# Strided attention into two feed-forward layers, one core: weights split in another way, and a new plan of the order

## Chip, cores, metric

One core of a Trainium2 chip runs the whole program. The metric is device time in microseconds for one execution.

## What is computed

Attention with 4 batches, 8 heads, 576 positions and head size 64: four heads look at the 32 latest positions, four at every 32nd earlier one. Its output, 2304 tokens of 512 numbers, goes through two feed-forward layers with 2048 hidden units each.

```python
scores = scale * np.matmul(q, k.transpose(0, 1, 3, 2))
mask_local = (rel >= 0) & (rel < stride)
mask_strided = (rel >= 0) & (pos[None, :] % stride == pos[:, None] % stride)
scores = np.where(masks[None, :, :, :], scores, -1000000000.0)
attn = np.exp(scores - np.max(scores, axis=-1, keepdims=True))
attn = attn / (np.sum(attn, axis=-1, keepdims=True) + 1e-09)
x = np.matmul(attn, v)                    # then laid out as 2304 x 512
h = x @ w_in;  x = (h * np.clip(h + 3.0, 0.0, 6.0) / 6.0) @ w_out
h = x @ w_in2; y = (h * np.tanh(np.log1p(np.exp(h)))) @ w_out2
```

Everything is float32; the weights are handed over as float64.

## The kernel before

**An order worked out beforehand.** The body adds its operations to a plan (class Plan, L103): each with an engine or a choice of engines, a cost in nanoseconds, what it depends on, and a due time. Plan.run (L171) is a list scheduler: again and again it takes the operation that can start first, and of those that can start at the same time the one that is due first (L199). Where an operation may run on several engines it takes the one on which it ends first, after a handicap (BIAS, FIRST_BIAS: 0 for GpSimd, 4000 ns for VectorE). Operations with a `lock` on an engine do not overlap in the plan (L192, L211). Then the instructions are issued in planned order (L862), so each engine works through its own queue in that order, whatever the true times are. The DMA loads are one queue, issued by SP.

**Fillers.** Up to FILL_UNTIL (L69, 20974 ns) of planned time, gaps of TensorE are filled with matmuls on zeros of FILL = 128 columns (fill, L155; L855 to L859), written to a bank that nothing uses then. Plan.stream (L143) halves TensorE's planned rate after stretches with few columns.

**Attention.** Work goes by pairs of heads, 4 a batch, 16 in all (attend, L467). For a pair: q, k and v are loaded (load_pair, L438; SP at L446 and L460); 76 small matmuls make the scores in two banks (L490); VectorE adds the masks while scaling, into tile e (L503); then the maximum (L529), its subtraction (L530, GpSimd or VectorE), exp on ScalarE (L531), the sum (L532), its reciprocal (L534), the product (L535, GpSimd or VectorE); TensorE transposes e (L543, L546: 8 matmuls); copies to pt; 72 small matmuls with v (L574); and the result is split into xh (ScalarE, L292) and xl (VectorE, L600). float32 matmuls count double in the trace: "x76" is 38 in the code. There are N_E = 2 tiles e, so the scores of a pair wait for the transposes of the pair but one before (e_free, L476, L512). The strided masks are twelve small loads on SP (L422).

**Feed-forward.** Products are made to full precision of three matmuls on rounded operands (mm3, L693): high x low parts and high x high. Tokens are in blocks of 512, 512, 512, 256 and 512; hidden units in 16 chunks of 128 a layer; GROUPS splits the chunks into groups of 4, 6, 6 and 6, 5, 5. A step is one chunk on one block: 4 mm3 into h, the nonlinearity (hard_swish L700, mish L712), its split into gh (L292) and gl (L792, GpSimd or VectorE), and 4 mm3 into the sums y. Block 0 needs batch 0 of the attention, block 1 batches 0 and 1, and so on, so attention runs in between in the first group.

**Weights.** A chunk has two halves (in and out), 64 halves in all, each 128 x 512 float64. decode (L630) makes from each a rounded float32 part w(0) and a rest w(1): sign away (L651, ScalarE or VectorE), clamp (L658), shift of the high word by 3 (L662), merge of sign and exponent (L667), rounding copy to w(0) (L292), then the power of two (L673), the low 9 bits of the high word (L677), those joined with the low word (L681), and their product with the power as w(1) (L685). There are 3 raw tiles, 3 wa, 2 wm and 8 slots for finished chunks (6 until attention has ended).

**Due times** (L360 to L367, L606 to L627): START is when the feed-forward part is to begin, UNIT the time that it allows for a pair in between, EARLY_X how long before its first use a batch is due, HALF_PACE the least distance between two halves' due times.

## Time and profile before

| | us |
|---|---|
| median of 3 runs | 890.5 (889.73 to 892.34) |
| profiled execution | 890.85 |
| its span, first to last instruction | 889.0 |

| engine | busy us | share | instructions |
|---|---|---|---|
| TensorE, matmuls | 871.2 | 98% | 6448 |
| VectorE | 567.7 | 64% | 978 |
| ScalarE | 492.4 | 55% | 923 |
| GpSimd | 265.3 | 30% | 223 |

Busy time of TensorE counts the fillers and matmuls at half clock in full. A row of a timeline is a run of like instructions of one engine: start, length, how many, and in square brackets the idle time before it with what ended it. "issue" there means that nothing which the profile shows was waited for. Times in the table of groups are busy time and the mean of one in nanoseconds.

### The profile page before, as it was taken

To read this page: it belongs to the slowest core of one execution; us is meant where nothing else is said; L and a number is where in the kernel's file an instruction comes from. 1 tells how busy PE (TensorE), PEld (TensorE's weight loads), DVE (VectorE), ACT (ScalarE), POOL (GpSimd) and SP (SyncE) were. 2 spreads that over 40 slices of the span, in tenths; PEclk is the share of its full clock that TensorE was granted. 3 is DMA by queue.
4 is the path that set the end of the run, shared out by engine and by line. 5 is a ranking of instruction groups with operands and counts; after the bars stand their busy time and mean duration, and the time that the engine had idled before them with its cause. 6 is when DMAs were issued, how large, how long until landed. Compare 5 with 4: busy or idle time off the path is not lost.

```text
span 889.0 us, 15898 instructions
## 1 busy us (share of the span) xinstructions
PE 871.2 (98%) x6448; PEld 730.8 (82%) x6448; DVE 567.7 (64%) x978; ACT 492.4 (55%) x923; POOL 265.3 (30%) x223
## 2 busy tenths in 40 slices
PE   9698999999999999999999999999999999999998
PEld 8476777888888988888898888888888888888887
DVE  6668667888521479822168888346888867555564
ACT  2344554654222244433245877788887778666674
POOL 3243434222222222244262432222222222222222
PEclk9689999999999999999999999999999999999999
DMA  7956653323100022300003112000221100000112
GB/s 231 240 167 172 184 148 90 93 94 115 48 1 1 1 72 94 103 17 1 1 25 94 48 48 72 0 2 24 71 72 48 48 1 1 0 36 13 48 47 72
DMA packets 20441, 58.73 MB, mean 66 GB/s; under 512 B 3344, under 2 KB 6032, under 8 KB 20368
## 3 DMA queue, kind: packets, MB, share of 16 engines
q1 hardware_dynamic: 20368, 57.72, 21.9%
q8 instruction: 50, 0.82, 0.4%
q14 instruction: 23, 0.19, 0.1%
HBM read 52.99 MB, written 4.72 MB: 65 GB/s over the span
## 4 chain that ended last, share of the span: by engine, by line
PE 93%; issue 2%; DMA 2%; DVE 1%; SPq 1%; POOL 1%; ACT 0%; POOLq 0%
PE bank L696 30%; PE bank L697 29%; PE bank L698 29%; PE bank L574 2%; PE bank L490 1%; DMA y<-in_qkv_dram 1%; DMA v<-in_qkv_dram 1%; PE bank L543 1%; PE bank L546 1%; POOL e L535 0%; SPq L422 0%; SPq L647 0%; POOL gl L792 0%; DVE y L830 0%; DVE wa L673 0%
## 5 line engine op out<-in xcount | busy, mean ns | idle before, releaser
L792 POOL TENSOR_TENSOR gl<-t,gh 128x512 fp32r<-128x512 f32 (+1 forms) x160 | 198.7, 1243 | 539.4 <-ACT gh L292 496.2
L696 PE MATMUL bank<-xh,w 128*128 128x512 f32 (+1 forms) x640 | 238.5, 373 | 0.5 <-DVE e L503 0.5
L696 PE MATMUL bank<-gh,w 128*128 128x512 f32 (+1 forms) x640 | 237.6, 371 | 0.0
L697 PE MATMUL bank<-xl,w 128*128 128x512 f32 (+1 forms) x640 | 237.4, 371 | 0.0
L697 PE MATMUL bank<-gl,w 128*128 128x512 f32 (+1 forms) x640 | 236.3, 369 | 0.8 <-POOL gl L792 0.8
L698 PE MATMUL bank<-xh,w 128*128 128x512 f32 (+1 forms) x640 | 236.2, 369 | 0.0
L698 PE MATMUL bank<-gh,w 128*128 128x512 f32 (+1 forms) x640 | 235.5, 368 | 0.0
L696 PEld LDWEIGHTS bank<-xh,w 128*128 128x128 f32 x640 | 121.0, 189 | 22.7 <-issue 1.2
L696 PEld LDWEIGHTS bank<-gh,w 128*128 128x128 f32 x640 | 120.4, 188 | 21.8 <-issue 0.7
L698 PEld LDWEIGHTS bank<-xh,w 128*128 128x128 f32 x640 | 121.0, 189 | 20.8
L698 PEld LDWEIGHTS bank<-gh,w 128*128 128x128 f32 x640 | 120.4, 188 | 20.8 <-issue 0.3
L697 PEld LDWEIGHTS bank<-xl,w 128*128 128x128 f32 x640 | 121.1, 189 | 19.9 <-DVE xl L600 0.5
L697 PEld LDWEIGHTS bank<-gl,w 128*128 128x128 f32 x640 | 120.5, 188 | 20.5 <-POOL gl L792 1.2
L707 DVE SCALAR_TENSOR_TENSOR t<-t,bank 128x512 f32<-128x512 f32 (+1 forms) x80 | 50.6, 634 | 135.1 <-ACT t L704 134.8
L704 ACT ACTIVATE t<-bank 128x512 f32<-128x512 f32 (+1 forms) x80 | 44.2, 555 | 149.9 <-PE bank L698 149.8
L292 ACT CAST gh<-t 128x512 fp32r<-128x512 f32 (+1 forms) x160 | 91.3, 572 | 42.8 <-DVE t L707 23.2
L735 DVE SCALAR_TENSOR_TENSOR t<-t,seed 128x512 f32<-128x512 f32 (+1 forms) x80 | 70.9, 887 | 62.8 <-ACT seed L724 62.0
L740 DVE SCALAR_TENSOR_TENSOR t<-t,seed 128x512 f32<-128x512 f32 (+1 forms) x80 | 58.4, 730 | 41.4 <-ACT t L737 41.2
L737 ACT ACTIVATE t<-t,offset 128x512 f32<-128x512 f32 (+1 forms) x80 | 54.4, 680 | 49.9 <-DVE t L735 49.7
L830 DVE TENSOR_TENSOR y<-bank,y 128x512 f32<-128x512 f32 (+1 forms) x80 | 49.7, 636 | 22.3 <-PE bank L698 21.4
L728 ACT ACTIVATE t<-bank 128x512 f32<-128x512 f32 (+1 forms) x80 | 44.3, 554 | 29.6 <-PE bank L698 27.3
L651 ACT ACTIVATE wa<-raw 128x512 f32<-128x512 f32 x64 | 43.1, 673 | 28.1 <-DMA raw<-in_wts_dram 19.0
(51 smaller groups left out, 839.2 us busy)
## 6 DMA issues: line engine op xcount, KB each, us to landing
raw<-in_wts_dram SPq DMA_DIRECT2D x64, 512.0 KB, 3.7
qk<-in_qkv_dram SPq DMA_DIRECT2D x15, 576.0 KB, 5.2
v<-in_qkv_dram SPq DMA_DIRECT2D x22, 256.0 KB, 4.7
out_dram<-y SPq DMA_DIRECT2D x16, 256.0 KB, 2.0
v<-in_qkv_dram SPq DMA_DIRECT2D x8, 288.0 KB, 5.2
y<-in_qkv_dram SPq DMA_DIRECT2D x1, 576.0 KB, 8.4
y<-in_qkv_dram SPq DMA_DIRECT2D x2, 256.0 KB, 7.9
out_dram<-y SPq DMA_DIRECT2D x4, 128.0 KB, 1.8
```

The lines of the kernel that those rows point to most:

```text
L292: nc.scalar.copy(out, src)
L696: nc.tensor.matmul(o, a[:, 1], high, start=first, stop=False)
L697: nc.tensor.matmul(o, a[:, 0], low, start=False, stop=False)
L698: nc.tensor.matmul(o, a[:, 0], high, start=False, stop=last)
L704: o = add("act", act_ns(n, True), lambda: nc.scalar.activation(t, h(), AF.Relu, bias=0.5, scale=1.0 / 6.0), [prod, free])
L707: lambda: nc.vector.scalar_tensor_tensor(t, t, 1.0, h(), ALU.min, ALU.mult), [o], frees=s.h,
L728: o = add("act", act_ns(n, True), lambda: nc.scalar.activation(t, h(), AF.Tanh, scale=0.5), [prod, free])
L735: lambda: nc.vector.scalar_tensor_tensor(t, t, 4.0, seed(), ALU.add, ALU.mult), [o], lock=("dve",),
L737: o = add("act", act_ns(n), lambda: nc.scalar.activation(t, t, AF.Square, bias=offset, scale=scale), [o])
L740: lambda: nc.vector.scalar_tensor_tensor(t, t, more, seed(), ALU.add, ALU.mult), [o], lock=("dve",),
L792: lambda eng, gh=gh, gl=gl, t=t: engines[eng].tensor_tensor(gl, t, gh.bitcast(F32), ALU.subtract),
L830: lambda y=y, src=src: nc.vector.tensor_tensor(y(), src(), y(), ALU.add), [op, *before], due=due, frees=bank,
```

## The change

1. decode: the mask of the rest is 0x3FFFFFFF instead of 0x3FFFF000, so the merged value keeps 20 bits of mantissa; w(0) is its rounding copy as before. The rest w(1) is now (merged value - w(0)) + low word x 2^-52 x power. Seven VectorE instructions become four (shift, merge, power, product); the clamp, the subtraction and the addition may run on GpSimd or VectorE.
2. The plan knows TensorE's instruction supply (late): instructions come in pieces of PIECE = 256, each is asked for at a fixed place and arrives SUPPLY = 6000 ns later; an operation that would run out is planned later. A filler counts 4 instructions, mm3 6, scores 152, transposes 16, values 144.
3. Fillers have 512 columns, until 60000 ns of planned time, and a tile of zeros of their own (640 columns).
4. The twelve strided mask loads are issued by ScalarE, due at 3000 ns.
5. N_E is 4; the scores no longer wait for a free e (the mask additions still do), and two of the e tiles get their unused columns cleared by GpSimd.
6. UNIT 1800 to 1200, HALF_PACE 7500 to 6263, EARLY_X 11000 to 8000.

```diff
-N_QKV, N_E, N_PT = 2, 2, 2
+N_QKV, N_E, N_PT = 2, 4, 2
-UNIT = 1800
-HALF_PACE = 7500
-EARLY_W, EARLY_G, EARLY_X = 8224, 12000, 11000
+UNIT = 1200
+HALF_PACE = 6263
+EARLY_W, EARLY_G, EARLY_X = 8224, 12000, 8000
-FILL, FILL_UNTIL = 128, 20974
+FILL, FILL_UNTIL = 512, 60000
+PIECE, ASKED, AHEAD, SUPPLY = 256, 140, 308, 6000
...
+    def late(self, t, op):
+        done, s = self.counted, 0.0
+        first, n = done[-1][0], op.count or 6
+        k = max(0, -(-(first - ASKED - AHEAD) // PIECE))
+        while (asked := ASKED + k * PIECE) + AHEAD < first + n:
+            if asked < first:
+                i = bisect.bisect_left(done, (asked, 0.0))
+                s = max(s, done[i][1] + SUPPLY - t - max(0, asked + AHEAD - first) / n * op.cost)
+            k += 1
+        return s
...
                     t = at[e]
+                    if e == "pe":
+                        t += self.late(t, op)
...
+    zeros = ap_.tile([P, P + FILL], F32, name="zeros")
...
-            return add("dma", 460, lambda: nc.sync.dma_start(mk_str[rows, slots], src))
+            return add("act", 420, lambda: nc.scalar.dma_start(mk_str[rows, slots], src), due=3000)
...
-        done = []
+        done = [add("pool", 150, lambda e=e: nc.gpsimd.memset(e[:, :, WS:], 0.0), due=12000) for e in e_t[NPAIR // 2:]]
...
-        s_op = add("pe", 900, scores, [src.qk, *e_free], bank=both)
+        s_op = add("pe", 900, scores, [src.qk], bank=both)
+        s_op.count = 4 * (4 * NB + 2)
...
         o = add(
-            "dve", dve_ns(DM / 2),
-            lambda: nc.vector.tensor_scalar(a, a, TINY, HUGE, ALU.max, ALU.min), [o], lock=("dve",),
+            None, {"dve": dve_ns(DM / 2), "pool": 50 + 1.05 * DM},
+            lambda eng: engines[eng].tensor_scalar(a, a, TINY, HUGE, ALU.max, ALU.min), [o], lock=("dve", "pool"),
         )
         o = add(
             "dve", dve_ns(DM / 2),
-            lambda: nc.vector.tensor_scalar(ai, ai, 3, 0x3FFFF000, ALU.logical_shift_left, ALU.bitwise_and),
+            lambda: nc.vector.tensor_scalar(ai, ai, 3, 0x3FFFFFFF, ALU.logical_shift_left, ALU.bitwise_and),
             [o], lock=("dve",),
         )
-        hi = add(
+        whole = add(
             "dve", dve_ns(DM),
             lambda: nc.vector.scalar_tensor_tensor(ai, high, 0xC0000000, ai, ALU.bitwise_and, ALU.bitwise_or),
             [o], lock=("dve",),
         )
-        o = add(None, copy_ns(DM), lambda eng: copy(eng, w(0), a), [hi, *old_w], lock=("dve",))
-        power = add(
-            "dve", dve_ns(DM / 2),
-            lambda: nc.vector.tensor_scalar(ai, ai, 0xFF800000, None, ALU.bitwise_and), [o], lock=("dve",),
-        )
+        hi = add(None, copy_ns(DM), lambda eng: copy(eng, w(0), a), [whole, *old_w], lock=("dve",))
         o = add(
             "dve", dve_ns(DM / 2),
-            lambda: nc.vector.tensor_scalar(resti, high, 0x1FF, None, ALU.bitwise_and), [load, old_m], lock=("dve",),
+            lambda: nc.vector.tensor_scalar(resti, ai, 0xFF800000, None, ALU.bitwise_and), [whole, old_m], lock=("dve",),
+        )
+        tail = add(
+            "dve", dve_ns(DM),
+            lambda: nc.vector.scalar_tensor_tensor(rest, low, 2.0 ** -52, rest, ALU.mult, ALU.mult), [o], lock=("dve",),
         )
         o = add(
-            "dve", dve_ns(DM),
-            lambda: nc.vector.scalar_tensor_tensor(rest, resti, 2.0 ** 32, low, ALU.mult, ALU.add), [o], lock=("dve",),
+            None, plain_ns(DM),
+            lambda eng: engines[eng].tensor_tensor(a, a, w(0).bitcast(F32), ALU.subtract), [hi, o], lock=("dve", "pool"),
         )
         lo = add(
-            "dve", dve_ns(DM),
-            lambda: nc.vector.scalar_tensor_tensor(w(1), rest, 2.0 ** -52, a, ALU.mult, ALU.mult),
-            [o, power, *old_w], lock=("dve",),
+            None, plain_ns(DM),
+            lambda eng: engines[eng].tensor_tensor(w(1), a, rest, ALU.add), [o, tail, *old_w], lock=("dve", "pool"),
         )
-        w_ops.append({"raw": [hi, o], "end": lo})
+        w_ops.append({"raw": [whole, tail], "end": lo})
...
-    zeros = t_t[0]
-    cleared = add("dve", 520, lambda: nc.vector.memset(zeros[:, :2 * P], 0.0), due=0)
+    cleared = add("dve", 520, lambda: nc.vector.memset(zeros, 0.0), due=0)
```

## Rows read from the trace of the kernel before

**Rows 1.** Page, slices of the span, granted clock of TensorE in tenths

```profile
PEclk9689999999999999999999999999999999999999
```

**Rows 2.** Stretches: length, busy us (instructions) of five engines, clock, DMA share, GB/s

```profile
0.00:29.00 29.00, 22.80 (x487) 21.00 (x491) 17.48 (x39) 7.69 (x14) 9.88 (x15) 0.98 0.81 227
29.00:52.90 23.90, 20.86 (x428) 16.11 (x425) 13.72 (x31) 9.41 (x22) 3.51 (x3) 0.53 0.71 201
52.90:100.00 47.10, 42.85 (x890) 33.41 (x889) 37.11 (x79) 25.89 (x57) 21.43 (x17) 1.00 0.64 185
...
100.00:884.00 784.00, 784.00 (x4652) 659.72 (x4651) 498.19 (x827) 449.44 (x832) 230.49 (x188) 1.00 0.16 49
```

**Rows 3.** Timeline of TensorE, saturated stretch: start, length, instructions

```profile
103.52 0.39 PE L696 MATMUL bank<-gh,w 128*128 128x512 f32 x1
...
104.20 0.60 PE L543 MATMUL bank<-mk,e 128*128 128x128 f32 x4
...
105.10 1.00 PE L490 MATMUL bank<-qk 64*32 64x54 f32 x76
...
106.93 1.25 PE L574 MATMUL bank<-pt,v 64*64 64x32 f32 x72
```

**Rows 4.** Timeline of TensorE, first 50 us

```profile
9.40 9.87 PE L857 MATMUL bank<-t 128*128 128x128 f32 x86
...
20.00 1.00 PE L490 MATMUL bank<-y 64*32 64x54 f32 x76
...
24.45 0.88 PE L574 MATMUL bank<-pt,v 64*64 64x32 f32 x42 [0.97 <-DMA v<-in_qkv_dram]
28.81 2.88 PE L574 MATMUL bank<-pt,v 64*64 64x32 f32 x98 [3.47 <-issue]
...
33.91 1.12 PE L543 MATMUL bank<-mk,e 128*128 128x128 f32 x4 [0.28 <-POOL e L535]
...
41.81 0.42 PE L574 MATMUL bank<-pt,y 54*64 54x32 f32 x2 [2.75 <-issue]
...
46.73 2.14 PE L574 MATMUL bank<-pt,v 54*64 54x32 f32 x72
```

**Rows 5.** Timeline of TensorE, around 70 us

```profile
69.08 0.31 PE L574 MATMUL bank<-pt,v 64*64 64x32 f32 x6 [1.26 <-issue]
69.90 0.50 PE L696 MATMUL bank<-xh,w 128*128 128x512 f32 x1 [0.51 <-DVE e L503]
```

**Rows 6.** Chain of waits (a landing), timelines of SP and ScalarE, first 20 us

```profile
3.12 8.38 DMA y<-in_qkv_dram
...
3.62 10.07 SPq L422 DMA_DIRECT2D mk_str<-in_masks_dram  x12
...
15.35 3.73 SPq L460 DMA_DIRECT2D v<-in_qkv_dram  x6
...
13.23 0.68 ACT L531 ACTIVATE e<-e 128x576 f32<-128x576 f32 x1 [2.85 <-POOL e L530]
```

**Rows 7.** Groups by line on VectorE, 0 to 100 us: three of decode's seven

```profile
L673 DVE TENSOR_SCALAR wa<-wa 128x512 uint32<-128x512 uint32 x8 | 6.5, 811 | 0.7 <-ACT w L292 0.7
...
L681 DVE SCALAR_TENSOR_TENSOR wm<-wm,raw 128x512 f32<-128x512 uint32 x8 | 5.5, 694 | 0.0
...
L662 DVE TENSOR_SCALAR wa<-wa 128x512 uint32<-128x512 uint32 x9 | 3.8, 417 | 0.0
```

**Rows 8.** Groups by line on GpSimd, whole span

```profile
L792 POOL TENSOR_TENSOR gl<-t,gh 128x512 fp32r<-128x512 f32 (+1 forms) x160 | 198.7, 1243 | 539.4 <-ACT gh L292 496.2 <-issue 34.7 <-PE bank L697 8.6
...
L726 POOL TENSOR_SCALAR seed<-seed 128x512 f32<-128x512 f32 x2 | 1.2, 618 | 5.2 <-ACT seed L731 5.2
```

**Rows 9.** Timelines of VectorE and GpSimd, 60 to 70 us

```profile
63.49 1.38 DVE L673 TENSOR_SCALAR wa<-wa 128x512 uint32<-128x512 uint32 x1
...
65.85 0.63 DVE L685 SCALAR_TENSOR_TENSOR w<-wm,wa 128x512 fp32r<-128x512 f32 x1
...
63.05 1.53 POOL L535 TENSOR_TENSOR e<-e,sum 128x576 f32<-128x576 f32 x1 [2.22 <-DVE sum L534]
```

More of the change, by code (lines that the diff above doesn't have):

```diff
@@ L1 @@
+import bisect
 import concourse.bass as bass
@@ L77 @@
 class Op:
-    __slots__ = ("engine", "costs", "cost", "emit", "deps", "due", "banks", "frees", "start", "end", "left", "users", "rows", "lock")
+    __slots__ = ("engine", "costs", "cost", "emit", "deps", "due", "banks", "frees", "start", "end", "left", "users", "rows", "lock", "count")
     def __init__(self, costs, emit, deps, due, bank, frees, lock=""):
@@ L92, in __init__ @@
         self.rows = 1.0
+        self.count = 0
         self.lock = lock
@@ L168, in fill @@
             t = free_bank[n] = op.end
+            n = self.counted[-1][0]
+            self.counted.extend([(n, op.start), (n + 4, op.end)])
         return done
     def run(self):
-        self.columns = {}
+        self.columns, self.counted = {}, [(0, 0.0)]
         free = dict.fromkeys(self.AFTER, ORIGIN)
@@ L210, in run @@
             free[e] = op.end
+            if e == "pe":
+                n = self.counted[-1][0]
+                self.counted.extend([(n, t), (n + (op.count or 6), op.end)])
             if e in op.lock:
@@ L852, in attention_then_two_ffns @@
     add("dve", 60, lambda: nc.vector.memset(offset, STEP[1]), due=1000)
-    zeros = t_t[0]
-    cleared = add("dve", 520, lambda: nc.vector.memset(zeros[:, :2 * P], 0.0), due=0)
+    cleared = add("dve", 520, lambda: nc.vector.memset(zeros, 0.0), due=0)
     plan.filler = cleared, 3 + 4 * FILL / 2.4, lambda n: nc.tensor.matmul(
-        banks[n][:, :FILL], zeros[:, :P], zeros[:, P:P + FILL], start=True, stop=True
+        banks[n][:, :FILL], zeros[:, :P], zeros[:, P:], start=True, stop=True
     )
```

4 lines of the change are left out of this document (3 added, 1 removed).

## Prediction

> **What bounds the kernel now.** I read the slices of the page first: the granted clock of TensorE drops in the second and third slice and nowhere else [rows 1]. The table by stretches comes next: from 100 to 884 us TensorE is busy for every microsecond at full clock, with VectorE and GpSimd at 64% and 29% [rows 2]. Whatever is taken off another engine there is worth nothing unless it makes TensorE wait. The question is how much useful TensorE work is done in the first 100 us.
>
> That needs prices at full clock, read where TensorE is saturated [rows 3]: the transposes of a pair take 0.90 us from start to start, a triple of 512-wide matmuls 0.68, and by their own rows the scores 1.00 and the values 1.25, so 3.15 us a pair. By 52.9 us the timeline holds six score groups (6.0), four transposes (3.6), four values (5.0) and six triples (4.1): 18.7 us of useful work, 34.2 lost. From 52.9 to 100 us TensorE is idle for 47.10 - 42.85 = 4.3 us [rows 2]. The loss is 38.5 us in all, and the forecast is what part of it comes back.
>
> Where it goes stands in the timeline of TensorE [rows 4]. Until 19 us fillers run, because the first pairs are in their softmax. The scores of pair 2 start at 20.00, right behind the transposes of pair 0, whose e tile they need (N_E is 2); those of pair 3 stand behind the transposes of pair 1. Then the values wait 0.97 us for v, and twice, 3.47 and 2.75 us, for "issue", which is no semaphore at all. The clock falls to 1.2 GHz with the first of these two and is back at 52.9 us (mean 0.53 in between) [rows 2]. The values of pair 3 end near 49 us, and only then does the feed-forward part run in earnest.
>
> What is "issue"? 478, 733 and 1242 matmuls stand before the rows that end such waits at 28.81, 41.81 and 69.08 [rows 4, 5]. With a weight load each, that is instruction 956, 1466 and 2484: steps of 510 and 1018, near twice and four times 256. All fall into groups of short matmuls, some 75 in 1.2 us. TensorE runs out of instructions there, at the pieces that the new planner calls PIECE. The Trainium skill ("Runtime: NRT & Kernel Launch", Instruction fetch mechanics) says that instructions come in blocks of 256 and that crossing a block's boundary is "mostly hidden". The spacing agrees with the block; the 3.47 and 2.75 us do not agree with hidden. By that rule the supply term below would be nothing, and rival B is what is left.
>
> **The change part by part.**
>
> Supply in the plan: the two early waits, 6.2 us, lie on the path; the plan now puts other work or a filler in front of such an instruction. Only the order is changed, so a piece that comes later than the planned 6 us still stalls TensorE. From instruction 652, in the scores at 20.00, to the restart at 28.81 are 8.3 us, if the plan has the places of the requests right. I credit both waits and keep 2 us of rest for each in the upper bound.
>
> Clock: in the cold 23.9 us TensorE is busy 20.9 us [rows 2]; the same work at the prices above (two scores 2.0, two transposes 1.8, 242 value matmuls 4.2, six triples 4.1) is 12.1. If no long wait occurs, 8.8 us of TensorE time come back.
>
> Four e tiles: scores 2 could start when q and k have landed (issued at 3.12, 8.38 us under way, so 11.5 [rows 6]) instead of at 20.00, scores 3 some microseconds later. Their softmax then runs beside that of pairs 0 and 1. A pair takes 13.9 us from its scores to its transposes (20.00 to 33.91 for pair 2 [rows 4]). With scores 3 near 15, their transposes come at 28 to 29, and x of batch 0 is whole near 32 instead of 50. The wait for a free e moves from TensorE's queue to VectorE's mask additions; behind those stand the weights, but with four tiles it is four pairs back and over. Two small GpSimd memsets more come before GpSimd has input.
>
> Masks to ScalarE's queue: SP needs 10.07 us for twelve issues, and the next loads, the v of pair 0 among them, stand behind (15.35 us) [rows 6]. Off SP, v lands before pair 0 needs it: the 0.97 us, inside the term for batch 0. No row shows a DMA issued by ScalarE. Twelve at the 0.62 us of SP's next six issues are 7.5 us; at SP's own 10.07 that is the other end. The sign of the first weight, ScalarE's first work, then slips by 4 to 8 us, at no cost, since no decoded weight is used before the values that start at 28.81 have ended; the exp at 13.23 is the first that would hurt [rows 4, 6]. I take the near end and zero, since 7.5 us end well before 13.23, and keep 2 us for the upper bound.
>
> Fillers: four instructions now cover 512 columns, so they use a quarter of the supply. One takes four times the 0.23 us of today (86 matmuls, two a filler, in 9.87 us [rows 4]), 0.9 us. Each that the plan places where TensorE is in truth late delays what is behind it by up to that: none or five of them, 0 to 4.5 us. I take 1. Their longer memset (640 columns instead of 256) lies ahead of the first loads' landing.
>
> Decode: seven VectorE instructions per half, between 0.81 us (L673) and 0.42 (L662) in the first 100 us, 4.3 in sum; dearest, cheapest and one of two inputs are shown [rows 7]. After it VectorE keeps the shift, the merge, the power and one product: 0.42 + 0.69 + 0.42 to 0.81 + 0.69, 2.2 to 2.6 us (power and shift are the same kind of instruction; L673 is dearer because it meets GpSimd, below). Clamp, subtraction and addition go to GpSimd at 0.62 + 1.24 + 1.24 = 3.1 us, by its own rows for such instructions [rows 8]. What decides is whether the two engines run side by side. They do not always: L673 takes 1.38 us while the softmax product runs on GpSimd (63.05, 1.53 us) [rows 9], against a mean of 0.81. The Trainium skill ("SBUF — State Buffer", SBUF: two separate sides) says that these engines share a port pair as an exclusive lock and that the loser waits for the whole instruction. The row agrees. By that rule moving work to GpSimd costs where it looks free, which is rival C.
>
> Counted as one resource, a half goes from 4.3 to 2.4 + 3.1 = 5.5 us. Near 33 us I expect halves 0 to 2 and pairs 0 to 3 done; five halves (27.5), five pairs at two GpSimd instructions of 1.24 (12.4) and three gl (3.7) remain before block 0 is fed: 43.6 us if nothing overlaps. Meanwhile TensorE has block 0 (4 chunks x 8 x 0.68 = 21.8) and five pairs (15.8), 37.6 us. So 6 us are lost to the weights there. From 100 us on I cost the 1.2 us more per half at nothing: both engines have free time [rows 2]. If that cover were gone at a change of groups, eight halves in a row would be 10 us late.
>
> HALF_PACE, UNIT and EARLY_X are due times alone: they decide ties. The first weights fall due up to 7 us later, attention 3. Nothing by itself.
>
> **Sum.** Lost after: to 32 us, 32 less four scores (4.0), four transposes (3.6), four values (5.0) and three triples (2.0) = 17.4; to 76 us, 6; later 0.5; long fillers 1. That is 25 against 38.5: 13.5 us less. The profiled execution took 890.85 us with a span of 889.0; the median of the runs is 890.5. I forecast 877.
>
> **Rivals.**
>
> A, the forecast: 871 to 883. Chance 0.55.
>
> B, the start keeps its shape: waits of 8 us, or others that the plan doesn't know, let the clock fall again, and the in-order queues pass every delay on. For it: 8.3 us against the planned 6. Then early scores and v bring 2 to 6 us: 884 to 889. Chance 0.20, of which 0.07 lies within 0.3%.
>
> C, slower: the shared port decides in the first 90 us. Half 4 is done at 66.5 (65.85 + 0.63) and used at 69.90 [rows 5, 9]: just in time. Eight halves at 1.2 us more are 10 us later, if VectorE has no idle time to give back. It decides once the 3.1 us per half no longer fall into GpSimd's idle time; 35 of the first 100 us are busy [rows 2]. With the 2 to 6 us of B off, 4 to 8 us slower: 895 to 899. Chance 0.09.
>
> D, the port does not bind and batch 0 is whole by 29 or 30 us: 15 + 2 + 0.5 lost, 21 less, 866 to 871. For it: not all these instructions collide. Chance 0.16.
>
> **How the numbers follow.** 0.3% (2.7 us) is about what measuring this kernel can tell from no change. Faster: 0.55 + 0.16 + 0.13 = 0.84. Within: 0.07. Slower: 0.09. The range 867 to 889 takes in A, B and most of D and leaves out C and the lowest of D, some 0.13.
>
> **What would show it.** Right: clock 1.00 through the first 100 us; "issue" waits of TensorE under 2 us in sum; scores 2 before 15 us and the values of pair 3 ended before 34; TensorE full from about 35 instead of 53; over 55 us of GpSimd busy in the first 100. Wrong: a second cold stretch (B); TensorE waiting for w or gl between 35 and 90 us (C); any wait of TensorE after 100 us, which is in none of my terms.

## The result, and the profile after

The changed kernel takes 896.2 us (median; 894.6 to 897.2) against 890.1 for the kernel before on the same chip: 1.0061 of it, 95% interval 1.0040 to 1.0082. So it is slower, by 6 us, where 877 was forecast. Its profiled execution took 897.15 us with a span of 895.4, 6.4 more than before.

The page of the changed kernel, granted clock of TensorE in 40 slices, against [rows 1]:

```profile
PEclk9899999999999999999999999999999999999999
```

Its table of stretches, with the columns of [rows 2]:

```profile
...
29.00:52.90 23.90, 21.49 (x494) 15.00 (x494) 17.07 (x33) 12.62 (x31) 19.61 (x15) 0.82 0.72 197
52.90:100.00 47.10, 46.04 (x971) 34.68 (x971) 35.23 (x68) 24.93 (x57) 41.10 (x30) 1.00 0.69 188
100.00:884.00 784.00, 775.84 (x4431) 647.95 (x4431) 491.78 (x648) 445.42 (x821) 495.54 (x347) 1.00 0.15 46
```

Two things stand out against [rows 2]. From 29 to 52.9 us the mean clock is 0.82 instead of 0.53: the stretch at 1.2 GHz is much shorter. And from 100 us on TensorE, which was busy for all of 784.00 us, now is busy for 775.84, while GpSimd has 495.5 us to do instead of 230.5.

The timeline of TensorE in the first 50 us of the changed kernel answers to [rows 4]. L517 are scores, L571 the first half of a pair's transposes, L603 values (L726 to L728 are the feed-forward part, L886 fillers):

```profile
15.32 0.82 PE L517 MATMUL bank<-y 64*32 64x54 f32 x61
...
24.33 0.66 PE L571 MATMUL bank<-mk,e 128*128 128x128 f32 x4 [1.38 <-POOL e L563]
...
26.85 1.29 PE L517 MATMUL bank<-qk 64*32 64x64 f32 x76 [1.49 <-DMA qk<-in_qkv_dram]
...
31.19 2.30 PE L603 MATMUL bank<-pt,v 64*64 64x32 f32 x144
...
36.49 0.66 PE L571 MATMUL bank<-mk,e 128*128 128x128 f32 x4 [0.45 <-POOL e L563]
...
38.51 1.23 PE L603 MATMUL bank<-pt,v 54*64 54x32 f32 x72
```

There is no long "issue" wait any more (the one of 0.30 us at 16.45 is the only one). Scores of pair 2 start at 15.32 instead of 20.00. But the transposes of pair 0 come at 24.33 and its values at 31.19. In the kernel before, the transposes of pair 0 came 5.2 us earlier:

```profile
19.10 0.60 PE L543 MATMUL bank<-mk,e 128*128 128x128 f32 x4
```

By the prices of [rows 3] the useful work by 52.9 us is six scores (6.0), five transposes (4.5), five values (6.3) and eight triples (5.4), 22.2 us: 30.7 lost instead of 34.2. To 100 us come 1.1 us of idle time and three fillers, 2.2 us from start to end: 34.0 lost instead of 38.5. At 100 us the changed kernel is 4.5 us ahead. The rest of the span gives away more than that: 10.9 us, as the whole span is 6.4 longer. The waits of TensorE from 100 to 890 us (what was waited for: us in total, times, longest):

```profile
PE bank L726 <- DVE t L774: 6.1, 8, 1.3
PE bank L726 <- DVE y L860: 1.3, 1, 1.3
PE bank L726 <- DVE t L737: 0.7, 2, 0.4
```

That view of before has no row. Of the 10.9 us lost from 100 us on, these are 8.1; the first matmul after such a wait also takes 0.50 us instead of 0.39, and the rest isn't resolved. All eleven wait for VectorE: t is the last step of a nonlinearity, y a sum that must leave its bank. What VectorE and GpSimd do in such a place stands in their timelines around the wait that ends at 676.08 us (VectorE first; L765, L770 and L774 are mish, L693 decode's shift, L689 its clamp):

```profile
670.84 0.69 DVE L770 SCALAR_TENSOR_TENSOR t<-t,seed 128x512 f32<-128x512 f32 x1 [1.06 <-ACT t L767]
674.60 0.82 DVE L693 TENSOR_SCALAR wa<-wa 128x512 uint32<-128x512 uint32 x1 [3.06 <-POOL wa L689]
675.35 0.67 DVE L774 SCALAR_TENSOR_TENSOR t<-t,bank 128x512 f32<-128x512 f32 x1
```

```profile
672.65 5.75 POOL L689 TENSOR_SCALAR wa<-wa 128x512 f32<-128x512 f32 x3
```

```profile
676.08 0.50 PE L726 MATMUL bank<-xh,w 128*128 128x512 f32 x1 [1.07 <-DVE t L774]
```

VectorE has all that L774 needs at 671.5 us, but ahead of it in its queue stands L693, the shift of a half whose clamp is the first of three that GpSimd does from 672.65 on. VectorE waits 3.06 us for it; L774, and TensorE behind it, wait along. Over the whole span VectorE waits 30.3 us in this way, in front of the shift (us busy, mean ns, idle time before):

```profile
L693 DVE TENSOR_SCALAR wa<-wa 128x512 uint32<-128x512 uint32 x64 | 60.6, 949 | 30.5 <-POOL wa L689 30.3
```

And a clamp is long. The groups by line on GpSimd, whole span:

```profile
L689 POOL TENSOR_SCALAR wa<-wa 128x512 f32<-128x512 f32 x64 | 131.3, 2056 | 20.5 <-ACT wa L682 15.7 <-DVE wa L684 4.0 <-PE bank L727 0.8
L716 POOL TENSOR_TENSOR w<-wa,wm 128x512 fp32r<-128x512 f32 x64 | 93.2, 1456 | 11.5 <-DVE wm L708 9.8 <-PE bank L728 0.6
L712 POOL TENSOR_TENSOR wa<-wa,w 128x512 f32<-128x512 f32 x64 | 92.3, 1444 | 27.4 <-ACT w L317 11.9 <-DVE wm L704 8.5 <-DVE xl L630 5.0
```

### The profile page after: what moved, and what is told of

It is laid out like the page before. It is cut to its first block, busy times and chain, and to the rows that moved or that the text cites. A ratio compares the mean times of both kernels' runs of the same rounds, so it can differ in the third digit from the quotient of the medians.

```text
span 895.4 us, 15780 instructions
## 1 busy us (share of the span) xinstructions
PE 871.9 (97%) x6368; PEld 716.4 (80%) x6368; DVE 561.0 (63%) x787; ACT 490.8 (55%) x923; POOL 577.2 (64%) x416
## 4 chain that ended last, share of the span: by engine, by line
PE 69%; DVE 8%; POOL 8%; ACT 7%; DMA 4%; issue 3%; ACTq 0%; SPq 0%; POOLq 0%
PE bank L726 22%; PE bank L727 21%; PE bank L728 21%; DMA raw<-in_wts_dram 2%; POOL wa L689 2%; POOL w L716 2%; DVE t L765 2%; POOL gl L822 2%; PE bank L603 1%; DVE t L770 1%; POOL wa L712 1%; DVE wm L708 1%; DMA qk<-in_qkv_dram 1%; PE bank L517 1%; ACT gh L317 1%
## 5 line engine op out<-in xcount | busy, mean ns | idle before, releaser
L822 POOL TENSOR_TENSOR gl<-t,gh 128x512 fp32r<-128x512 f32 (+1 forms) x160 | 201.2, 1258 | 241.8 <-ACT gh L317 220.8
L726 PE MATMUL bank<-xh,w 128*128 128x512 f32 (+1 forms) x640 | 239.9, 375 | 7.3 <-DVE t L774 6.1
L726 PE MATMUL bank<-gh,w 128*128 128x512 f32 (+1 forms) x640 | 238.4, 373 | 1.3 <-DVE y L860 1.3
L728 PE MATMUL bank<-xh,w 128*128 128x512 f32 (+1 forms) x640 | 235.8, 368 | 0.0
L728 PE MATMUL bank<-gh,w 128*128 128x512 f32 (+1 forms) x640 | 235.5, 368 | 0.0
L726 PEld LDWEIGHTS bank<-xh,w 128*128 128x128 f32 x640 | 120.5, 188 | 34.1 <-DVE t L774 9.5
L689 POOL TENSOR_SCALAR wa<-wa 128x512 f32<-128x512 f32 x64 | 131.3, 2056 | 20.5 <-ACT wa L682 15.7
L726 PEld LDWEIGHTS bank<-gh,w 128*128 128x128 f32 x640 | 120.4, 188 | 24.2 <-DVE y L860 2.0
L728 PEld LDWEIGHTS bank<-xh,w 128*128 128x128 f32 x640 | 120.7, 189 | 20.9
L728 PEld LDWEIGHTS bank<-gh,w 128*128 128x128 f32 x640 | 120.4, 188 | 20.7
L765 DVE SCALAR_TENSOR_TENSOR t<-t,seed 128x512 f32<-128x512 f32 (+1 forms) x80 | 80.5, 1007 | 60.7 <-ACT seed L754 59.8
L712 POOL TENSOR_TENSOR wa<-wa,w 128x512 f32<-128x512 f32 x64 | 92.3, 1444 | 27.4 <-ACT w L317 11.9
L716 POOL TENSOR_TENSOR w<-wa,wm 128x512 fp32r<-128x512 f32 x64 | 93.2, 1456 | 11.5 <-DVE wm L708 9.8
L734 ACT ACTIVATE t<-bank 128x512 f32<-128x512 f32 (+1 forms) x80 | 44.2, 553 | 87.3 <-PE bank L728 87.1
L770 DVE SCALAR_TENSOR_TENSOR t<-t,seed 128x512 f32<-128x512 f32 (+1 forms) x80 | 64.8, 810 | 42.8 <-ACT t L767 42.7
```

The source lines that it names most:

```text
L689: lambda eng: engines[eng].tensor_scalar(a, a, TINY, HUGE, ALU.max, ALU.min), [o], lock=("dve", "pool"),
L712: lambda eng: engines[eng].tensor_tensor(a, a, w(0).bitcast(F32), ALU.subtract), [hi, o], lock=("dve", "pool"),
L716: lambda eng: engines[eng].tensor_tensor(w(1), a, rest, ALU.add), [o, tail, *old_w], lock=("dve", "pool"),
L726: nc.tensor.matmul(o, a[:, 1], high, start=first, stop=False)
L728: nc.tensor.matmul(o, a[:, 0], high, start=False, stop=last)
L734: o = add("act", act_ns(n, True), lambda: nc.scalar.activation(t, h(), AF.Relu, bias=0.5, scale=1.0 / 6.0), [prod, free])
```

## Experiments

Theory C' (mine after the result): the clamp on GpSimd takes over three times what plan and prediction took for it, and that alone makes TensorE wait after 100 us; the start gains less than forecast because pair 0 comes late. Rivals: three more instructions a half are too many for the two engines whatever they are; or the new order of the start is to blame for all. "The old decode" below means item 1 of the change undone. Lost time is counted as above.

### The decode

**e1**: the changed kernel with the old decode.

```diff
-            None, {"dve": dve_ns(DM / 2), "pool": 50 + 1.05 * DM},
-            lambda eng: engines[eng].tensor_scalar(a, a, TINY, HUGE, ALU.max, ALU.min), [o], lock=("dve", "pool"),
+            "dve", dve_ns(DM / 2),
+            lambda: nc.vector.tensor_scalar(a, a, TINY, HUGE, ALU.max, ALU.min), [o], lock=("dve",),
...
```

> The changed kernel with the weights decoded as before: seven VectorE instructions, nothing on GpSimd; supply in the plan, long fillers, masks on ScalarE, four e tiles and the new due times stay. Theory P (GpSimd's share of decode costs, by its own length and by what it does to VectorE): TensorE's 8 us of idle time after 100 us go, the softmax of the first pairs is no longer behind clamps on GpSimd, so 880 to 886. Theory O (the new due times and the new order make TensorE wait, not the engine of the decode): the waits after 100 us stay, 892 to 897.

Measured: 887.3 us (883.5 to 889.3), 0.9947 [0.9926, 0.9969]. Everything but the decode makes the kernel faster, by 3.7 us. The table of stretches, and two waits of its TensorE timeline:

```profile
100.00:880.00 780.00, 779.64 (x4528) 656.17 (x4526) 493.43 (x820) 449.49 (x825) 228.43 (x185) 1.00 0.16 48
```

```profile
32.84 0.43 PE L517 MATMUL bank<-qk 64*32 64x64 f32 x16 [3.00 <-issue]
...
56.38 0.25 PE L517 MATMUL bank<-qk 64*32 64x54 f32 x1 [1.36 <-issue]
```

TensorE is full after 100 us again; the time is 1.3 us above the range of theory P. In this order, though, two waits for instructions are back that the plan had meant to avoid.

**e4**: the kernel before with item 1 alone.

```diff
-            "dve", dve_ns(DM / 2),
-            lambda: nc.vector.tensor_scalar(a, a, TINY, HUGE, ALU.max, ALU.min), [o], lock=("dve",),
+            None, {"dve": dve_ns(DM / 2), "pool": 50 + 1.05 * DM},
+            lambda eng: engines[eng].tensor_scalar(a, a, TINY, HUGE, ALU.max, ALU.min), [o], lock=("dve", "pool"),
...
```

> The kernel before with the new decode alone. Theory P: it is slower than before, by the 12 us that the changed kernel loses after 100 us and by a later start: 898 to 905. Theory O: VectorE has less to do in the start, where it was just in time, and the order stays as tuned: 884 to 890.

Measured: 908.1 us, 1.0181 [1.0159, 1.0203]. So the loss is the new decode's, on the old plan even more (3 us above the range of theory P). Waits of TensorE from 100 us on:

```profile
PE bank L696 <- DVE t L744: 5.8, 6, 2.2
PE bank L696 <- DVE y L830: 3.0, 1, 3.0
...
```

**e2**: the changed kernel with the clamp on VectorE only.

```diff
-            None, {"dve": dve_ns(DM / 2), "pool": 50 + 1.05 * DM},
-            lambda eng: engines[eng].tensor_scalar(a, a, TINY, HUGE, ALU.max, ALU.min), [o], lock=("dve", "pool"),
+            "dve", dve_ns(DM / 2),
+            lambda: nc.vector.tensor_scalar(a, a, TINY, HUGE, ALU.max, ALU.min), [o], lock=("dve",),
```

> The changed kernel with the clamp kept on VectorE; subtraction and addition may still go to GpSimd. The clamp took 2.06 us on GpSimd where 0.62 was reckoned with. Theory P1 (the clamp's length is the main harm): GpSimd's busy time falls by 131 us, 884 to 889. Theory P2 (any use of GpSimd beside VectorE harms alike): two instructions of 1.45 us a half stay, 890 to 894. Theory O: 892 to 897.

Measured: 891.6 us, 1.0010 [0.9996, 1.0023]. TensorE is busy for all of 780.00 us from 100 to 880, but 8 us worse off than the changed kernel at 100 us: the plan orders the start differently, the mean clock from 52.9 to 100 us is 0.86. The time lies in the range of theory P2, but not by its mechanism, as TensorE doesn't wait after 100 us. The run shows where the waits come from and not what the clamp costs, since two things changed.

**e6** keeps the order: the instructions of the changed kernel, one by one, with the clamp's maximum and minimum replaced by a product with 1 and a sum with 0 (the clamp is left out).

```diff
-            lambda eng: engines[eng].tensor_scalar(a, a, TINY, HUGE, ALU.max, ALU.min), [o], lock=("dve", "pool"),
+            lambda eng: engines[eng].tensor_scalar(a, a, 1.0, 0.0, ALU.mult, ALU.add), [o], lock=("dve", "pool"),
```

> The changed kernel, same plan and same order of every instruction, with the clamp's maximum and minimum replaced by times 1 plus 0 (the clamp itself is left out). On GpSimd the row of such a multiply-and-add is 0.62 us, that of the clamp 2.06. Theory L (the clamp's own length on GpSimd, not the use of GpSimd as such, makes TensorE wait after 200 us): GpSimd is 80 to 90 us less busy, the waits after 200 us go, 884 to 888. Rival (subtraction and addition collide with VectorE alike): waits of 5 us or more stay after 200 us, 890 to 895. Second rival (GpSimd takes 2 us for any two-operation instruction on this tile): no change, 895 to 898.

Measured: 884.3 us (881.6 to 886.6), 0.9931 [0.9909, 0.9953]: 11.9 us less than the changed kernel with the same order on every engine. Its group by line on GpSimd, and its stretch after 100 us:

```profile
L689 POOL TENSOR_SCALAR wa<-wa 128x512 f32<-128x512 f32 x64 | 49.4, 775 | 28.8 <-ACT wa L682 19.8 <-DVE wa L684 4.2 <-PE bank L574 3.4
```

```profile
100.00:880.00 780.00, 779.77 (x4559) 655.94 (x4541) 466.12 (x653) 448.62 (x826) 425.87 (x350) 1.00 0.15 47
```

The place that answers to the wait above, in the timelines of VectorE and of GpSimd:

```profile
663.97 0.83 DVE L693 TENSOR_SCALAR wa<-wa 128x512 uint32<-128x512 uint32 x1 [0.51 <-POOL wa L689]
664.72 0.67 DVE L774 SCALAR_TENSOR_TENSOR t<-t,bank 128x512 f32<-128x512 f32 x1
```

```profile
662.81 2.46 POOL L689 TENSOR_SCALAR wa<-wa 128x512 f32<-128x512 f32 x3
```

The three instructions take 2.46 us instead of 5.75, and VectorE waits 0.51 instead of 3.06; over the span its waits in front of the shift fall from 30.3 us to 2.7. The start has no part in the gain: at 100 us e6 has lost 0.8 us more than the changed kernel. So in this order the loss after 100 us is the 1.3 us more that a clamp takes on GpSimd. The subtraction and the addition stay there in e6, at 1.44 and 1.42 us, and cost nothing after 100 us.

**e16**: e4 with the same replacement (the clamp is left out).

```diff
-            lambda eng: engines[eng].tensor_scalar(a, a, TINY, HUGE, ALU.max, ALU.min), [o], lock=("dve", "pool"),
+            lambda eng: engines[eng].tensor_scalar(a, a, 1.0, 0.0, ALU.mult, ALU.add), [o], lock=("dve", "pool"),
```

> The kernel before with the new decode alone, which took 908.1 us against 890.9, but with the clamp's maximum and minimum replaced by a product with 1 and a sum with 0 (the clamp is left out); order and engines stay the same. Theory 'the loss of the new decode is the length of the clamp on GpSimd': the time falls to 889 to 897, TensorE's waits for the nonlinearity after 100 us from 9 us to under 2. Rival 'three instructions more a half on GpSimd are too many, the clamp or not': 900 to 908.

Measured: 893.4 us, 1.0028 [1.0014, 1.0043]. That is 14.7 us less than e4, which had lost some 17: most of the loss on the old plan is the clamp's length, too. TensorE waits 0.2 us after 100 us; the 2.2 us that are left lie in the start.

**e13**: the changed kernel, with 1900 ns for a clamp on GpSimd in the plan instead of 588.

```diff
-            None, {"dve": dve_ns(DM / 2), "pool": 50 + 1.05 * DM},
+            None, {"dve": dve_ns(DM / 2), "pool": 1900},
```

> The changed kernel with one number different: the plan reckons 1900 ns for a clamp on GpSimd instead of 588 (the runs of it took 1.92 to 2.06 us). Theory 'the plan was made with a wrong price': with the right one the clamps go where there is time, TensorE's waits after 100 us fall from 8.2 us to under 2 in sum, and the median is 884 to 889. Rival 'GpSimd has too much to do whatever the plan knows': most clamps move to VectorE (GpSimd busy under 520 us instead of 577), the start is as with all clamps on VectorE, and the time is 890 to 894.

Measured: 894.8 us (891.9 to 896.3), 1.0047 [1.0030, 1.0064]. Its two stretches after 52.9 us:

```profile
52.90:100.00 47.10, 42.41 (x800) 30.90 (x801) 33.28 (x66) 19.58 (x47) 34.56 (x28) 0.89 0.63 176
100.00:880.00 780.00, 780.00 (x4534) 655.48 (x4533) 473.80 (x651) 449.72 (x833) 498.94 (x352) 1.00 0.15 47
```

All 64 clamps are still on GpSimd (2.03 us each), yet TensorE doesn't wait once after 100 us, and VectorE waits in front of the shift for 11.5 us instead of 30.3:

```profile
L693 DVE TENSOR_SCALAR wa<-wa 128x512 uint32<-128x512 uint32 x64 | 53.3, 834 | 11.5 <-POOL wa L689 11.5
```

So theory C' says too much with "alone": GpSimd's load is as large here as in the changed kernel, and a long clamp makes TensorE wait where the order was planned with a short one. The plan orders the start anew as well: at 100 us this kernel has lost 6 us more than the changed one. In the profiled execution, the fastest of the four, it is 5.3 us ahead all the same; the median lies 3 us higher, and no trace shows where. The first theory was right on the waits and wrong on the time; the rival had the clamps move to VectorE, which they didn't, and was closer on the time.

### The start

**e3**: the changed kernel with the strided masks back on SP's queue.

```diff
-            return add("act", 420, lambda: nc.scalar.dma_start(mk_str[rows, slots], src), due=3000)
+            return add("dma", 460, lambda: nc.sync.dma_start(mk_str[rows, slots], src))
```

> The changed kernel with the twelve mask loads back on SP. Theory M (masks on ScalarE hold up the start: the local mask is loaded at 4.47 us instead of 1.65, ScalarE is held until 8.46): the local mask is loaded near 1.65 again, the first pair's masks are added near 9 instead of 12 us, and the total falls by 1 to 3 us, 893 to 895. Rival: v falls behind the masks again and the start is no earlier; 896 to 899.

Measured: 903.2 us, 1.0147 [1.0113, 1.0181]; 7 us slower than the changed kernel and above both ranges. Pair 0 is transposed at 19.25 us, but then TensorE waits 1.1 us for v and 3.7 for pt, and the clock is at 0.77 from 29 to 52.9 us. An early pair 0 alone makes no early start. In the profiled execution only 1.6 us of the difference is there at 100 us; most of it comes after 500 us, where TensorE's waits for VectorE are longer (10.2 us from 100 us on, against 8.1). So the start's share of the move is some 2 us. That the rest comes of clamps that fall in other places is likely and not tested.

**e8**: e1 with the strided masks planned behind the local ones.

```diff
-            return add("act", 420, lambda: nc.scalar.dma_start(mk_str[rows, slots], src), due=3000)
+            return add("act", 420, lambda: nc.scalar.dma_start(mk_str[rows, slots], src), local_load, due=12000)
```

> The changed kernel with the weights decoded as before, and with ScalarE's twelve mask loads planned behind the load of the local mask, so that the first SP loads are not behind them. Against 887 with the masks first. Theory M (masks at the head of ScalarE hold the first loads of SP back, 4.63 instead of 1.65 us for the local mask): the local mask and the q and k of pair 1 are issued by 3 us again, pair 0's masks are added before 10 us instead of 11, its transposes come 1 to 3 us earlier than 24, total 882 to 886. Rival: the first weights or v hold pair 0 all the same, 886 to 889.

Measured: 892.3 us, 1.0018 [1.0003, 1.0033], 5 us slower than e1 and above both ranges. The local masks go out at 1.17 instead of 4.63 us and pair 0 is transposed at 22.46 instead of 23.99, but now ScalarE is held in the middle of its work, and the scores of pair 4 wait 4.8 us for q and k. The issues in ScalarE's timeline:

```profile
4.40 9.99 ACTq L451 DMA_DIRECT2D mk_str<-in_masks_dram  x12
```

**e15**: e1 without the twelve loads; GpSimd writes zeros to their tile (the strided mask is left out).

```diff
-            return add("act", 420, lambda: nc.scalar.dma_start(mk_str[rows, slots], src), due=3000)
+            return add("act", 420, lambda: nc.gpsimd.memset(mk_str[rows, slots], 0.0), due=3000)
```

> The changed kernel with the old decode, and the twelve strided mask loads left out: GpSimd writes zeros to that tile instead, so the strided heads are computed without their mask. ScalarE is then free from the start, and no queue carries these loads; the order of TensorE, VectorE and SP is the same. Beside it stands the same kernel with the loads on ScalarE's queue, 887.3 us. Theory 'the twelve loads hold the start wherever they stand': pair 0 is transposed by 20 to 21 us instead of 24, and the median is 881 to 885. Rival 'what is gained before 50 us is given back to weights that come just in time': pair 0 is as early, but the time is 886 to 889.

Measured: 885.2 us (883.7 to 886.0), 0.9932 [0.9917, 0.9947]. The product of pair 0 (L563), the last step of its softmax, ends on GpSimd at 19.74 us, 4.0 us before e1's. But TensorE transposes the pair only at 22.11, 1.9 us before e1 and 3 us later than the kernel before, because long fillers, planned for a late pair 0, stand ahead of it in the queue:

```profile
18.20 1.54 POOL L563 TENSOR_TENSOR e<-e,sum 128x576 f32<-128x576 f32 x1 [3.25 <-DVE sum L562]
```

```profile
16.85 5.42 PE L886 MATMUL bank<-zeros 128*128 128x512 f32 x12
```

The medians differ by 2.1 us, the ranges overlap, and at 100 us the two profiled executions stand within 0.4 us. So in this order the loads cost some 2 us; what they cost in an order that is planned without them, no run shows. The time lies just outside both ranges.

**e17**: e1 with the loads issued by GpSimd.

```diff
-            return add("act", 420, lambda: nc.scalar.dma_start(mk_str[rows, slots], src), due=3000)
+            return add("pool", 420, lambda: nc.gpsimd.dma_start(mk_str[rows, slots], src), due=3000)
```

> The changed kernel with the old decode, and the twelve strided mask loads issued by GpSimd instead of ScalarE (887.3 us there; 885.2 with the loads left out). Theory 'the loads cost as much as they hold an engine that the softmax needs': ScalarE's first exp comes near 13.5 us as without the loads; if GpSimd has sent them before the first subtraction is ready (by 12 us), the median is 884 to 887. Rival 'the twelve issues take 8 to 10 us on any queue': GpSimd reaches its copies of the local mask and the first subtraction late, pair 0 is transposed at 24 us or later, and the time is 887 to 893.

Measured: 886.2 us (884.8 to 887.9), 0.9956 [0.9940, 0.9971], not to be told from e1. (With this edit the plan also moves the first weight's sign from VectorE to ScalarE.) GpSimd needs until 9.4 us for the twelve issues, the copies of the local mask stand behind them (9.62 us against 6.42 in e15), and the first subtraction comes at 14.69. The time is the theory's, the reason isn't: exp comes at 15.98, no earlier than in e1 (15.33), though pair 0 is transposed at 21.82. e1 and e17 are the two orders here that compute everything and beat the kernel before, by some 4 us.

**e5**: the changed kernel without the supply rule.

```diff
-                        t += self.late(t, op)
+                        t += 0.0
```

> The changed kernel whose plan leaves the instruction supply out; all else, the decode on GpSimd too, as changed. Theory S (the supply term in the plan is what keeps TensorE from running out of instructions; the changed kernel has one such wait of 0.3 us in the first 100 us): waits for issue of 3 to 8 us in sum come back before 100 us, 898 to 903. Rival: the earlier scores and the four e tiles alone spread the short matmuls, waits for issue stay under 2 us, 893 to 898.

Measured: 903.5 us, 1.0142 [1.0112, 1.0172], 7.3 us slower than the changed kernel. At 100 us 4.3 us more are lost; what is beyond that isn't resolved, since the clamps fall differently again. Waits of TensorE for instructions in the first 100 us, 4.4 us instead of 0.30:

```profile
PE bank L517 <- issue: 2.4, 2, 1.7
...
PE bank L603 <- issue: 1.0, 2, 0.7
PE bank L886 <- issue: 1.0, 1, 1.0
```

The clock falls three times, and its mean from 52.9 to 100 us is 0.93 instead of 1.00. The third fall follows a wait of 2.2 us for pt, so it can't be put down to the instructions.

**e11**: e1 with two e tiles and the old wait for a free one.

```diff
-N_QKV, N_E, N_PT = 2, 4, 2
+N_QKV, N_E, N_PT = 2, 2, 2
...
-        s_op = add("pe", 900, scores, [src.qk], bank=both)
+        s_op = add("pe", 900, scores, [src.qk, *e_free], bank=both)
```

> The changed kernel with the old decode and two e tiles as before, scores waiting for a free e again; all else changed. Against 887 with four. By the prediction's step on the e tiles, scores 2 and 3 fall back behind the transposes, x of batch 0 is later, 892 to 897. Rival E (four tiles bring scores forward that nothing waits for, among them those of pair 4): no slower, 884 to 888.

Measured: 892.6 us, 1.0021 [1.0003, 1.0040]. Pair 0 is transposed at 21.84, 2 us before e1, and the scores of pair 2 at 22.74; the four tiles are worth 5.3 us.

**e14**: e1 with the old due times.

```diff
-UNIT = 1200
-HALF_PACE = 6263
-EARLY_W, EARLY_G, EARLY_X = 8224, 12000, 8000
+UNIT = 1800
+HALF_PACE = 7500
+EARLY_W, EARLY_G, EARLY_X = 8224, 12000, 11000
```

> The changed kernel with the old decode and with the three old due times (UNIT 1800, HALF_PACE 7500, EARLY_X 11000). Beside it stands the same kernel with the new due times, 887.3 us. Theory 'due times alone do nothing': 886 to 889, lost TensorE time by 100 us within 2 us of it. Rival 'the new due times give attention and weights a better order in the first 100 us': 890 to 895. Second rival 'the new due times start the feed-forward part too early and so spoil the start': 882 to 885.

Measured: 891.0 us, 0.9998 [0.9985, 1.0010], 3.7 us slower than e1. TensorE waits 6.0 us for instructions in the first 100 us against 4.4 in e1, the clock falls again (0.93 from 52.9 to 100 us), and at 100 us 6 us more are lost than in e1.

**e7**: e1 with the short fillers.

```diff
-FILL, FILL_UNTIL = 512, 60000
+FILL, FILL_UNTIL = 128, 20974
```

> The changed kernel with the weights decoded as before on VectorE, and with fillers of 128 columns until 20974 ns as before. Against 887 with the long fillers. Theory F (each long filler that stands before ready work costs up to 0.9 us, and seven stand after 20 us): 883 to 886. Rival G (the fillers between 20 and 60 us keep the clock up): the cold stretch grows from 6.8 us to over 15 us and the total to 889 to 894.

Measured: 889.7 us, 0.9998 [0.9983, 1.0013]: 2.4 us slower than e1, with waits of 2.23, 1.86 and 2.06 us for instructions at 24, 101 and 116 us. The long fillers gain, but not where they stand: by 100 us both kernels have lost the same within 0.3 us, by 200 us e7 has lost 5 us more.

**e9** and **e10**: e2 and e1 with the scores of pairs 4 and on planned behind the values of the pair four before, since the scores of pair 4 (26.85 us above) stand ahead of the values of pair 0.

```diff
-        s_op = add("pe", 900, scores, [src.qk], bank=both)
+        s_op = add("pe", 900, scores, [src.qk, *(pairs[kk - 4].values if kk >= 4 else [])], bank=both)
```

> The changed kernel with the clamp on VectorE, and with the scores of a pair planned behind the values of the pair four before. In the changed kernel and in every run of it so far the scores of pair 4 stand in TensorE's queue ahead of the values of pair 0 and wait there for q and k, 1.5 to 4.8 us. Against 891.5 with the clamp on VectorE alone. Theory Q (these scores hold up the start): the waits of scores for q and k after 20 us go, values of pair 0 start by 27 us instead of 31, 884 to 888. Rival W (the weights and the shared port set the start, not the place of these scores): waits move elsewhere, 889 to 893.

> The same hold of the scores on the changed kernel with the old decode (887 without the hold). There the scores of pair 4 wait for instructions (3.0 us at 32.8) ahead of the values of pair 1. Theory Q: 882 to 886. Rival: the wait for instructions comes at the next group of short matmuls instead, 886 to 889.

Measured: 892.6 us, 1.0021 [1.0003, 1.0039], and 887.6 us, 0.9960 [0.9944, 0.9976]; without it 891.6 and 887.3. In e9 the values of pair 0 come at 26.44 us instead of 32.57, but waits for instructions take their place (3.03 and 2.00 us): no gain. e10 tests nothing: in e1 the scores of pair 4 (28.99 us) stand behind the values of pair 0 (25.94) already, and in the traces every engine of e10 has the instructions of e1 in the same order. So it is e1 once more, and shows that the waits for instructions vary in one order: 3.00 and 1.36 us in e1, 1.59 and 2.05 in e10.

**e12**: e10 with 8000 ns for a piece of instructions.

```diff
-PIECE, ASKED, AHEAD, SUPPLY = 256, 140, 308, 6000
+PIECE, ASKED, AHEAD, SUPPLY = 256, 140, 308, 8000
```

> As the second of these (old decode, held scores), with 8000 ns instead of 6000 for a piece of instructions in the plan. Theory T (the plan is short by the 2 us that a piece takes longer while loads run): waits for issue under 1 us in the first 100 us, the clock stays up longer, 880 to 884. Rival: the plan gives away more than it saves, and the total is that of the run with 6000 or up to 3 us above.

Measured: 900.3 us, 1.0105 [1.0074, 1.0136], above both ranges. The waits for instructions are gone (0.5 us), and at 52.9 us this kernel has lost less than any other here, 2.7 us less than the changed one. Then, in its timeline of TensorE:

```profile
65.15 0.80 PE L726 MATMUL bank<-gh,w 128*128 128x512 f32 x1 [3.36 <-DVE w L715]
...
111.02 1.83 PE L603 MATMUL bank<-pt,v 54*64 54x32 f32 x72 [3.70 <-ACT pt L317]
```

TensorE runs into a weight and a pt that aren't ready, and the clock falls again (0.89 from 52.9 to 100 us, 0.95 to 200). What a start gains is given back when weights or pt are just in time; the runs don't tell what start would be the best.

## Why the prediction was wrong

**The decode: the step that failed.** It took 0.62 us for a clamp on GpSimd, from the page's only tensor-scalar instruction there [rows 8], which isn't a maximum and minimum, and 1.24 for the two others. They took 2.06, 1.44 and 1.46: 5.0 us a half instead of 3.1. The mis-sized term is the clamp above all; in the order of the changed kernel e6 prices its excess at 11.9 us of the time. Nothing bounded it from above: a duration from a near row was taken for a duration of that operation.

**"From 100 us on ... at nothing"** failed with it. That both engines had free time [rows 2] was true of the mean, and was enough in e6 and e13. What decides is who stands behind whom: the shift on VectorE now waits for another engine, and the nonlinearity, which TensorE needs at once, is queued behind the shift. I named nobody behind that new wait. The wrong price stands in the plan, too (588 ns), and so the plan put the shift where the clamp would have been done; with a truer price (e13) VectorE waits there for 11.5 us instead of 30.3, and TensorE not at all. The sentence with a price for lost cover, 10 us, had the size of what happened by luck: it meant weights that come late, and what came late was the nonlinearity.

**VectorE** was to keep 2.2 to 2.6 us a half. In the first 100 us, by line (us busy, mean ns), against [rows 7]:

```profile
L708 DVE SCALAR_TENSOR_TENSOR wm<-raw,wm 128x512 f32<-128x512 uint32 x9 | 10.3, 1141 | 0.0
...
L698 DVE SCALAR_TENSOR_TENSOR wa<-raw,wa 128x512 uint32<-128x512 uint32 x9 | 7.5, 837 | 0.0
...
L693 DVE TENSOR_SCALAR wa<-wa 128x512 uint32<-128x512 uint32 x9 | 5.8, 645 | 3.7 <-POOL wa L689 3.7
L704 DVE TENSOR_SCALAR wm<-wa 128x512 uint32<-128x512 uint32 x9 | 5.6, 622 | 0.0
```

That is 3.2 us, and VectorE's busy time over the span is 561.0 us against 567.7: three instructions a half fewer, and 6.7 us saved in all. L708 takes 1.14 us in the mean where L681, of the same form, took 0.69; the shortest L708 of the span takes 0.63. The Trainium skill ("SBUF — State Buffer", SBUF: two separate sides) says that VectorE, in an instruction with two inputs among others, and GpSimd share a port pair as an exclusive lock, and that the loser waits out the other's whole instruction. The longer mean agrees, though no row shows what an instruction of VectorE waited for inside its own time.

**Rival C** had the size (895 to 899) and GpSimd beside VectorE as the resource, but the wrong place and mechanism, so that 896 lies in its range is luck. Between 35 and 90 us TensorE waits 0.5 us for w. The loss is after 200 us, in the nonlinearity, which my last sentence named as "in none of my terms".

**The supply** was right: both waits are gone, and without the rule 4.4 us of such waits come back (e5). The Trainium skill ("Runtime: NRT & Kernel Launch", Instruction fetch mechanics) calls such a crossing "mostly hidden"; e1's 3.00 us and e5 don't agree. The rule doesn't serve every order: with the old decode it leaves waits of 3.00 and 1.36 us (e1), 1.59 and 2.05 in the second run of that order (e10).

**The clock** came back in part: 0.82 instead of 0.53, not the 1.00 forecast.

**Four e tiles** gave scores 2 at 15.32 and scores 3 at 16.63, as forecast near 15. But the 13.9 us from a pair's scores to its transposes were read where two pairs were under way. With four, pair 2 took from 15.32 to 33.42 and pair 3 from 16.63 to 36.49, 18 to 20 us, and I left pair 0 where it was although it shares its queues with them. By 32 us I had counted 14.6 us of useful work and there were 7.6 (five scores, two transposes, the first of the values): 7.0 us of the 9.0 that the start fell short of its 13.5. The values of pair 3 end at 39.7, not before 34. That the tiles gain stands (e11, 5.3 us).

**Masks on ScalarE**, taken at zero, cost some 2 us in the order of e1 (e15), by a way that I hadn't looked at. Timelines of ScalarE, of SP and of GpSimd in the changed kernel:

```profile
0.73 7.69 ACTq L448 DMA_DIRECT2D mk_str<-in_masks_dram  x12
8.46 1.28 ACT L317 ACT_TABLE_LOAD   x1 [8.46 <-DMA mk_str<-in_masks_dram]
...
17.46 0.68 ACT L559 ACTIVATE e<-e 128x576 f32<-128x576 f32 x1 [5.21 <-POOL e L558]
```

```profile
4.47 0.33 SPq L435 DMA_DIRECT2D mk<-in_masks_dram  x1
6.45 0.33 SPq L473 DMA_DIRECT2D qk<-in_qkv_dram  x1
```

```profile
10.51 1.27 POOL L712 TENSOR_TENSOR wa<-wa,w 128x512 f32<-128x512 f32 x1 [0.38 <-POOL mk_loc L440]
11.73 0.23 POOL L443 COPY mk_loc<-mk 128x64 f32<-128x64 f32 x1
...
20.02 1.92 POOL L689 TENSOR_SCALAR wa<-wa 128x512 f32<-128x512 f32 x1 [1.03 <-ACT wa L682]
21.90 1.27 POOL L712 TENSOR_TENSOR wa<-wa,w 128x512 f32<-128x512 f32 x1
23.12 1.16 POOL L563 TENSOR_TENSOR e<-e,sum 128x576 f32<-128x576 f32 x1
```

The 7.69 us were within my bounds. But SP, whose twelve issues were gone, sends the local masks at 4.47 us where they follow on its first loads at 1.66 in e15, and q and k of pair 1 at 6.45 instead of 2.13. In between it waits 2.9 us for the first weights to land and 1.6 for a mask; with GpSimd as the issuer (e17) the local masks go out at 1.66 again, and why, the runs don't show. And on GpSimd decode's instructions stand between those of the softmax: a subtraction (L712) ahead of the last copy of the local mask, a clamp and a subtraction ahead of the product L563 of pair 0. So pair 0's exp comes at 17.46 us instead of 13.23 [rows 6].

GpSimd's part in this counts for less than it seems. In e1, with nothing of decode on GpSimd, exp comes at 15.33 us, 2.1 sooner, but the transposes of pair 0 at 23.99, only 0.3 sooner. There a weight's sign stands on ScalarE between pair 0's exp and its sum, and waits for its load:

```profile
20.30 0.69 ACT L681 ACTIVATE wa<-raw 128x512 f32<-128x512 f32 x1 [4.29 <-DMA raw<-in_wts_dram]
```

Off SP, where they had held it for 10.07 us, the twelve loads still are better placed than on it, by 1.6 us at 100 us (e3).

**Fillers** were to cost 1 us and gain 2.4 (e7), by waits for instructions that they spare after 100 us; where a pair is ready early they hold it up, by 2.4 us in e15. **Due times**, "nothing by itself", gain 3.7 (e14): they decide where a weight stands in front of a softmax, in the very stretch on which the rest of the sum was built.

So the start's terms taken together were of the right sign, and the part that arrived is 3.7 us with the old decode, 6.3 with a cheap clamp, not 13.5.

## What to carry to other kernels

An operation moved to another engine is priced by a row of that very operation there; where none exists, its upper bound is a multiple (here it was 3.3 times) and belongs in the sum, as a list scheduler turns a wrong price into an order that makes others wait. Free time on both engines doesn't make a move free: name what is queued, on the engine that stays, behind the instruction that now waits for the other. And a start built from many coupled queues gives back much of what one wait removed: here a quarter to a half of what was counted arrived.

## What the runs showed of the hardware

- On GpSimd, a maximum and minimum with two constants on 128x512 float32 takes 1.91 us at least and 2.06 in the mean; a product and a sum with two constants, the same shape, 0.78 in the mean.
- Twelve small loads hold the engine that issues them for 7.7 us (ScalarE, from the start), 10.0 (ScalarE, from 4.4 us on; SP before) and until 9.4 us (GpSimd). Issued by ScalarE from the start they delay SP's third load from 1.66 us to 4.47; issued by GpSimd they don't. ScalarE's table load of 1.28 us stood behind them, at 8.46 us.
- The granted clock falls again as late as 100 us and more: in e12 TensorE waits 3.70 us for pt until 111.02, and the 72 values behind that take 1.83 us instead of 1.25, the matmuls 0.63 instead of 0.39, at 1.2 GHz.
